# Attention and two feed-forward layers on one core: the work beside the attention in one chunk of 512 tokens per batch instead of two of 288

## The chip, the cores and the metric

The kernel runs on one core of a Trainium2 chip. TensorE multiplies matrices, ScalarE and VectorE evacuate its results, GpSimd works on data in on-chip memory, and SyncE's queue issues nearly all transfers. The metric is the time of one execution on the device in microseconds (us).

## What is computed

Four batches of 576 tokens go through attention with 8 heads of 64, with a decay bias, and then through two feed-forward layers (512 to 2048 to 512) for all 2304 tokens. Cut to what matters:

```python
scores = scale * np.matmul(q, k.transpose(0, 1, 3, 2))
scores = np.where(causal, -1000000000.0, scores + np.minimum(bias, 0.0))
attn = softmax(scores)
x = (attn @ v).transpose(0, 2, 1, 3).reshape(2304, 512)
h = x @ moe_w_in;   x = np.maximum(0.01 * h, h) @ moe_w_out
h = x @ moe2_w_in;  out = (np.maximum(h, 0) + np.log1p(np.exp(-np.abs(h)))) @ moe2_w_out
```

## The kernel before

Every operand of the feed-forward layers is split into a high and a low part, so that a product takes three matmuls. The weights arrive as 64-bit numbers and are loaded and split block by block (`load_w`, `split_w`): a block is 128 of the 2048 inner features, `i` for the first matrix of a layer and `o` for the second. The pool of split weights has 8 places for each kind, and block 8 takes the place of block 0.

The 16 blocks of a layer are worked through in 4 groups of G = 4. The first group of the first layer is special: most of its work is done beside the attention.

The attention works on 16 pairs of heads (four for each batch) in 64 units of scores, four to a pair: rows 384 to 511 (512 columns of scores), the last 64 rows (288), rows 256 to 383 (384), and rows 0 to 255 (256 and 128). They run through a software pipeline. Step n of the loop in `attention` issues the scores of unit n + 1 on TensorE, the maxima and exponentials of unit n, the normalization of unit n - 1 on GpSimd, and the transposes of unit n - 2 on TensorE (`pt_t`) with their evacuation to PA, PZ or PB. In the first and third step of a pair's four (n = 4p, 4p + 2) `pv` multiplies with V (`pt_v`) and splits the result into xh and xl. After the last scores, steps 63 to 66 drain the pipeline.

The class `Fill` holds a queue of units of feed-forward work. When a batch is through the attention, `ready` appends its units; `step` calls `run` in every step of the loop, between the two halves of the transposes, and `run` issues at most one unit: `h` (12 matmuls into `ps_h` for one block) or `o` (12 matmuls into `ps_o` for 128 of the 512 outputs, over the group's four blocks), if the weights and the inputs that it needs are there. A unit's result is evacuated by ScalarE (`gf`, then `gh`) and GpSimd (`gl`), or by ScalarE (`o`), which SyncE's queue stores to `part` in device memory. All units during the attention share one bank of the accumulation memory. From step 64 on, `run` is called more often, and after the loop until the queue is empty.

Then comes the main part: a list of steps, each with an `h` unit for one block and one chunk of tokens, and the output matmuls (`ps_out`) of three steps before. Its first group does what the Fill queue has left, that is the last batch; the next groups work on all tokens in chunks of 512, 512, 256, 512 and 512. `load_acc` brings the stored results of the first group back.

Of the kernel before, what the change touches and what calls it, by code (L numbers as in the profile page):

```python
# [9 lines left out]
F32 = mybir.dt.float32  # L10
I32 = mybir.dt.int32
U32 = mybir.dt.uint32
F32R = mybir.dt.float32r
# [4 lines left out]
P = 128  # L18
NEG = -8.0e9
G = 4  # L20
# [10 lines left out]
def attn_moe_moe(ctx, tc, q, k, v, s, w1i, w1o, w2i, w2o, out):  # L31
    nc = tc.nc

    B, H, S = s.shape
    D = v.shape[-1]
    NT, DM = out.shape
    DFF = w1i.shape[1]
    KD = DM // P
    NF = DFF // P
# [2 lines left out]
    NP = B * NPAIR  # L42
    NB = S // P
    TL = S - NB * P
    CW = S // 2
    scale = 1.0 / float(D) ** 0.5

    nc.scalar.preload_act_table_set("natural_log_exp_and_others")
# [1 line left out]
    def pool(name, bufs=1, **kw):  # L50
        return tc.tile_pool(name=name, bufs=bufs, **kw)

    dram = ctx.enter_context(pool("dram", space=bass.MemoryType.DRAM))
# [4 lines left out]
    xh = keep.tile([P, KD, NT], F32R, tag="xh", name="xh")  # L58
    xl = keep.tile([P, KD, NT], F32R, tag="xl", name="xl")
    bb_d = dram.tile([B * H, 2, S], F32R, tag="bb_d", name="bb_d")  # L60
    part = dram.tile([2 * B, P, KD, CW], F32, tag="part", name="part")


    todo = {}
# [2 lines left out]
    def later(n, fn, *args):  # L67
        todo.setdefault(clock[0] + n, []).append((fn, args))
# [12 lines left out]


    wt, wio = {}, {}
    wpool = ctx.enter_context(pool("wpool", bufs=2 * G))
    wio["tmp"] = ctx.enter_context(pool("wtmp", bufs=2))

    def load_w(layer, f, nm, place=None):
# [10 lines left out]

    def split_w(layer, f, nm, at):

        raw = wt.pop((layer, f, nm, "raw"))
        L, Hw = raw[:, :, 0], raw[:, :, 1]
        m = wio["tmp"].tile([P, DM], I32, tag="wm", name="wm")
        t = wio["tmp"].tile([P, DM], I32, tag="wt", name="wt")
        nc.scalar.activation(m.bitcast(F32), Hw.bitcast(F32), AF.Abs)
        nc.scalar.activation(t, L.bitcast(U32), AF.Copy, scale=2.0 ** -29)

        mf = m.bitcast(F32)

        def clamp():  # L110
            nc.vector.tensor_scalar(mf, mf, D_MIN, D_MAX, op0=ALU.max, op1=ALU.min)

        def shift():
            nc.vector.tensor_scalar(m, m, 3, 0x3FFFFFFF, op0=ALU.logical_shift_left, op1=ALU.bitwise_and)

        def sign():
            nc.vector.scalar_tensor_tensor(m, Hw, -0x40000000, m, op0=ALU.bitwise_and, op1=ALU.bitwise_or)  # L117

        def add():
            nc.gpsimd.tensor_tensor(m, m, t, op=ALU.add)  # L120

        def high():
            hi = wpool.tile([P, DM], F32R, tag=f"w{nm}h", name=f"w{nm}h")
            nc.scalar.activation(hi, m.bitcast(F32), AF.Copy)
            wt[layer, f, nm] = [hi]

        def low():
            lo = wpool.tile([P, DM], F32R, tag=f"w{nm}l", name=f"w{nm}l")
            hi = wt[layer, f, nm][0]
            nc.gpsimd.tensor_tensor(lo, m.bitcast(F32), hi.bitcast(F32), op=ALU.subtract)  # L130
            wt[layer, f, nm].append(lo)

        for n, fn in zip(at, (clamp, shift, sign, add, high, low)):
            later(n, fn)


    def h_mm(ps, layer, f, xh, xl):
        hi, lo = wt[layer, f, "i"]
        n = 0
        for kk in range(KD):  # L140
            w = slice(kk * P, (kk + 1) * P)
            for a, b in ((hi[:, w], xh[:, kk, :]), (hi[:, w], xl[:, kk, :]), (lo[:, w], xh[:, kk, :])):
                nc.tensor.matmul(ps, a, b, start=n == 0, stop=n == 3 * KD - 1)  # L143
                n += 1
# [307 lines left out]
    class Fill:  # L452
# [19 lines left out]
        def step(self, n):  # L472
            if n == 4 * NPAIR + 1:
                self.begin()
            if n in self.loads:
                (f, nm), place = self.loads[n]
                load_w(0, f, nm, wio[place])
            if n - 3 in self.loads:
                split_w(0, *self.loads[n - 3][0], (1, 2, 3, 4, 5, 6))
            self.run()  # L480

        def bank(self, nm):

            tag, bufs = ("m", 1) if not self.free else self.free.pop(0)
            if self.free is not None:
                self.free.append((tag, bufs))
            return self.ps.tile([P, 512], F32, tag=tag, name=nm, bufs=bufs)[:, :CW]

        free = None

# [7 lines left out]
                fn(*args)  # L498

        def ready(self, b):  # L500
            hs, os = [], []
            for ch in range(2):
                c0 = b * S + ch * CW
                x = xh[:, :, c0:c0 + CW], xl[:, :, c0:c0 + CW]
                gs = {}
                hs += [(self.h, (f, x, gs)) for f in range(G)]
                os += [(self.o, (dm, 2 * b + ch, gs)) for dm in range(KD)]

            self.units += hs[:G + 1] + os[:KD] + hs[G + 1:] + os[KD:]

        def h(self, f, x, gs):
            ps = self.bank("ps_h")
            h_mm(ps, 0, f, *x)
            new = lambda pool, nm, dt=F32: pool.tile([P, CW], dt, tag=nm, name=nm)

            def leaky():
                gf = new(self.tpool, "gf")
                nc.scalar.activation(gf, ps, AF.Prelu, alpha=0.01)
                later(1, high, gf)

            def high(gf):
                gh = new(self.gpool, "gh", F32R)
                nc.scalar.activation(gh, gf, AF.Copy)
                later(1, low, gf, gh)

            def low(gf, gh):
                gl = new(self.gpool, "gl", F32R)
                nc.gpsimd.tensor_tensor(gl, gf, gh.bitcast(F32), op=ALU.subtract)
                gs[f] = gh, gl

            later(1, leaky)

        def o(self, dm, c, gs):
            ps = self.bank("ps_o")
            w = slice(dm * P, (dm + 1) * P)
            for f in range(G):
                (wh, wl), (gh, gl) = wt[0, f, "o"], gs[f]
                for n, (a, b) in enumerate(((wh, gh), (wh, gl), (wl, gh))):
                    nc.tensor.matmul(ps, a[:, w], b, start=f == 0 and n == 0, stop=f == G - 1 and n == 2)  # L539

            def store():
                o = self.tpool.tile([P, CW], F32, tag="o", name="o")
                nc.scalar.activation(o, ps, AF.Copy)  # L543
                nc.sync.dma_start(part[c, :, dm, :], o)

            later(1, store)

    with pool("psA", bufs=2, space=PSUM) as psA:
# [11 lines left out]
            tick()  # L560
        fill.stack.close()

    for nm in "io":
        wio[nm] = ctx.enter_context(pool("raw" + nm))
    acc = ctx.enter_context(pool("accpool")).tile([P, KD, NT], F32, tag="acc", name="acc")

    def load_acc(c):
        nc.sync.dma_start(acc[:, :, c * CW:(c + 1) * CW], part[c])


    gpool = ctx.enter_context(pool("gpool", bufs=4, side="right"))
# [2 lines left out]
    ps_o = ctx.enter_context(pool("ps_o", bufs=5, space=PSUM))  # L574

    chunks = [(0, 512), (512, 512), (1024, NT - 2048), (NT - 1024, 512), (NT - 512, 512)]
    first = [((B - 1) * S + ch * CW, CW) for ch in range(2)]
    groups = [(layer, g) for layer in range(2) for g in range(NG)]
    steps = []
    for layer, g in groups:  # L580
# [17 lines left out]
    gs = {}  # L598
# [80 lines left out]
    for gi, (layer, g) in enumerate(groups[1:]):  # L679
        a, z = start[groups[gi]], start[layer, g]  # L680
        when = [(a + n - 1, a + n) for n in (0, 3, 6, 8, 11, 14, 16, 19)] if gi else [None] * 4 + [(0, 2), (1, 4), (3, 6), (5, 8)]
        for j, at in enumerate(when):
            if at:
                f, nm = divmod(j, 2)
                w = (layer, g * G + f, "io"[nm])
                plan.setdefault(at[0], []).append((load_w, w))
                plan.setdefault(at[1], []).append((split_w, (*w, (1, 1, 1, 1, 2, 2))))
    for c in range(2 * (B - 1)):
        plan.setdefault(2 * c + 2, []).append((load_acc, (c,)))

    for n, (layer, g, c, is_first, is_last, f) in enumerate(steps):
        N = c[1]
        cols = slice(c[0], c[0] + N)
        ps = ps_h.tile([P, 512], F32, tag="h", name="ps_h")
        h_mm(ps[:, :N], layer, g * G + f, xh[:, :, cols], xl[:, :, cols])
        tick()
        settle()
        act1(n, layer, N, ps)
        for fn, w in sorted(plan.pop(n, ()), key=lambda x: (split_w, load_w, load_acc).index(x[0])):
            fn(*w)  # L700
        if n >= LAG:
            out_mm(n - LAG)
# [52 lines left out]
```

## Time and profile before

| what | value |
|---|---|
| median of 3 runs | 997.46 us (996.87 to 997.95) |
| the profiled execution: time, span | 996.73 us, 995.0 us |
| TensorE busy | 974.7 us, 98% of the span |
| ScalarE, VectorE, GpSimd busy | 539.2, 526.5, 571.9 us |
| granted clock of TensorE | 1.00 |

A matmul is pipelined: a 512-wide one lasts 390 ns in the profile, while the next one starts after less. So what a stretch costs TensorE is read from the starts of its instructions.

### The profile page before, as it was taken

Reading aid. Unit: us, or ns where it says so; the run is one execution under the profiler, and the core shown is the slowest. Engines: PE = TensorE matmul, PEld = TensorE weight load, DVE = VectorE, ACT = ScalarE, POOL = GpSimd, SP = SyncE. Lnnn points to the kernel's source line nnn. Section 1 sums busy time; section 2 is a strip of 40 time slices with the busy share of each in tenths; the row PEclk is TensorE's granted clock in tenths of the full one; section 3 lists DMA queues with packets and bytes.
Section 4 is the critical chain, followed back from the end, with each engine's and each line's share of the span. In section 5 each row is a group of like instructions: output and inputs, shape, how many; then the busy total and the mean of one; then the engine's idle time right before and its main releaser. Section 6 shows DMA issues by size and latency. Waiting matters only on the chain.

```text
span 995.0 us, 15234 instructions
## 1 busy us (share of the span) xinstructions
PE 974.7 (98%) x5498; PEld 810.8 (81%) x5498; DVE 526.5 (53%) x1133; ACT 539.2 (54%) x1152; POOL 571.9 (57%) x565
## 2 busy tenths in 40 slices
PE   6889999999999999999999999999999999999998
PEld 4667788888898888888888888888888888888886
DVE  6886665545122322132215437767687868763534
ACT  4877766756355333334334546776657655654452
POOL 6757545543256444444444446777867776775553
PEclk9999999999999999999999999999999999999999
DMA  5422324221163111111111111111111111100202
GB/s 176 135 89 80 112 86 132 71 78 32 37 198 127 43 43 43 43 43 43 47 38 43 44 43 42 43 43 43 43 43 43 43 42 43 43 1 1 85 22 85
DMA packets 38519, 62.05 MB, mean 62 GB/s; under 512 B 2932, under 2 KB 25972, under 8 KB 38444
## 3 DMA queue, kind: packets, MB, share of 16 engines
q1 hardware_dynamic: 38204, 60.74, 18.6%
q8 instruction: 44, 0.72, 0.3%
q10 hardware_dynamic: 240, 0.33, 0.1%
q14 instruction: 31, 0.25, 0.1%
HBM read 52.65 MB, written 8.40 MB: 61 GB/s over the span
## 4 chain that ended last, share of the span: by engine, by line
PE 91%; DVE 3%; ACT 3%; issue 1%; POOL 1%; DMA 1%; SPq 0%; ACTq 0%; POOLq 0%; DVEq 0%
PE ps_h L143 40%; PE ps_out L657 36%; PE pt_v L354 4%; PE ps_o L539 4%; PE pt_s L262 3%; PE pt_t L323 3%; PE pt_s L252 1%; ACT sc L295 1%; DVE sc L281 1%; PE pt_t L318 1%; DMA V<-in_v 0%; DVE st L286 0%; ACT PA L335 0%; DVE acc L667 0%; ACT PB L335 0%
## 5 line engine op out<-in xcount | busy, mean ns | idle before, releaser
L150 POOL TENSOR_TENSOR gl<-gf,gh 128x512 fp32r<-128x512 f32 (+2 forms) x148 | 181.1, 1224 | 138.8 <-ACT gh L149 129.1
L143 PE MATMUL ps_h<-xh,wih 128*128 128x512 f32 (+2 forms) x688 | 245.6, 357 | 1.1 <-ACT o L543 0.6
L143 PE MATMUL ps_h<-xl,wih 128*128 128x512 f32 (+2 forms) x688 | 243.8, 354 | 0.0
L143 PE MATMUL ps_h<-xh,wil 128*128 128x512 f32 (+2 forms) x688 | 243.8, 354 | 0.0
L667 DVE TENSOR_TENSOR acc<-ps_out,acc 128x512 f32<-128x512 f32 (+1 forms) x114 | 73.7, 662 | 164.4 <-PE ps_out L657 164.4
L622 POOL TENSOR_TENSOR t<-e,t 128x512 f32<-128x512 f32 (+1 forms) x80 | 112.4, 1406 | 72.0 <-DVE t L621 71.3
L306 POOL TENSOR_SCALAR sc<-sc,st 128x512 f32<-128x512 f32 (+4 forms) x160 | 88.2, 563 | 103.0 <-DVE st L302 60.5
L143 PEld LDWEIGHTS ps_h<-xh,wih 128*128 128x128 f32 x688 | 129.6, 188 | 19.8 <-ACT o L543 0.8
L143 PEld LDWEIGHTS ps_h<-xl,wih 128*128 128x128 f32 x688 | 129.6, 188 | 17.9
L143 PEld LDWEIGHTS ps_h<-xh,wil 128*128 128x128 f32 x688 | 129.5, 188 | 17.6
L606 ACT ACTIVATE gf<-ps_h 128x512 f32<-128x512 f32 (+2 forms) x68 | 36.6, 538 | 170.0 <-PE ps_h L143 169.4
L657 PE MATMUL ps_out<-woh,gl 128*128 128x512 f32 x288 | 112.3, 390 | 0.0
L657 PE MATMUL ps_out<-woh,gh 128*128 128x512 f32 x288 | 112.3, 390 | 0.0
L657 PE MATMUL ps_out<-wol,gh 128*128 128x512 f32 x288 | 112.2, 390 | 0.0
L149 ACT ACTIVATE gh<-gf 128x512 fp32r<-128x512 f32 (+2 forms) x148 | 85.5, 578 | 49.3 <-DVE gf L632 48.6
L295 ACT ACTIVATE sc<-sc,st 128x512 f32<-128x512 f32 (+2 forms) x144 | 83.4, 581 | 42.2 <-DVE st L286 21.2
L120 POOL TENSOR_TENSOR wm<-wm,wt 128x512 int32<-128x512 int32 x64 | 85.0, 1329 | 31.3 <-DVE wm L117 31.3
L657 PE MATMUL ps_out<-gh,wol 128*128 128x512 f32 (+2 forms) x272 | 97.8, 359 | 0.0
L657 PE MATMUL ps_out<-gh,woh 128*128 128x512 f32 (+2 forms) x272 | 97.7, 359 | 0.0
L657 PE MATMUL ps_out<-gl,woh 128*128 128x512 f32 (+2 forms) x272 | 97.7, 359 | 0.0
L281 DVE CUSTOM_DVE_ANT_0 sc<-pt_s,mask 128x512 f32<-128x512 f32 (+2 forms) x144 | 66.7, 480 | 57.0 <-PE pt_t L323 46.0
L621 DVE TENSOR_SCALAR t<-e 128x512 f32<-128x512 f32 (+1 forms) x80 | 44.3, 554 | 98.0 <-ACT e L612 98.0
(93 smaller groups left out, 1731.7 us busy)
## 6 DMA issues: line engine op xcount, KB each, us to landing
rawi<-in_moe_w_in SPq DMA_DIRECT2D x32, 512.0 KB
rawo<-in_moe_w_out SPq DMA_DIRECT2D x32, 512.0 KB
V<-in_v SPq DMA_DIRECT2D x16, 320.0 KB
Q<-in_q SPq DMA_DIRECT2D x15, 320.0 KB
K<-in_k SPq DMA_DIRECT2D x16, 288.0 KB
out<-acc SPq DMA_DIRECT2D x18, 256.0 KB
part<-o SPq DMA_DIRECT2D x24, 144.0 KB
acc<-part SPq DMA_DIRECT2D x6, 576.0 KB
```

The lines of the kernel that those rows point to most:

```text
L120: nc.gpsimd.tensor_tensor(m, m, t, op=ALU.add)
L143: nc.tensor.matmul(ps, a, b, start=n == 0, stop=n == 3 * KD - 1)
L149: nc.scalar.activation(gh, gf, AF.Copy)
L150: nc.gpsimd.tensor_tensor(gl, gf, gh.bitcast(F32), op=ALU.subtract)
L281: nc.vector.tensor_tensor_reduce(out=self.sc[:, j, c], in0=self.ps[j][:, c], in1=m, scale=-scale, scalar=3.0e38, op0=ALU.add, op1=ALU.min, ...
L295: nc.scalar.activation(x, x, AF.Exp, scale=-1.0, bias=self.stat(0, e), accum_out=self.stat(1, e))
L306: nc.gpsimd.tensor_scalar(x, x, self.stat(2, e), 1.0, op0=ALU.mult, op1=ALU.mult)
L354: nc.tensor.matmul(pt[j * D:(j + 1) * D, o:o + w], V[p % 2][:, c, j, :], x[:, j, :], start=m == 0 or (not last and m == 1), stop=m == len( ...
L621: nc.vector.tensor_scalar(t, e, 1.0, -1.0, op0=ALU.add, op1=ALU.add)
L622: nc.gpsimd.tensor_tensor(t, e, t, op=ALU.subtract)
L657: nc.tensor.matmul(ps, a, b, start=f == 0 and m == 0, stop=f == G - 1 and m == 2)
L667: nc.vector.tensor_tensor(d, o, d, op=ALU.add)
```

## The change

A batch's turn at the Fill queue is one chunk of 512 tokens instead of two of 288: chunk b is the tokens 512 b to 512 b + 511, released when batch b is through. Three batches release 24 units of 512 instead of 48 of 288. The main part's first group takes the 768 tokens that are left, in two chunks of 384, instead of 576 in two of 288. Tiles of the units grow from 288 to 512 columns. The pool of split weights becomes two, of six places and of two; the second is made only behind the attention. Each block has the same turn among 8 places as before.

```diff
-    CW = S // 2
+    FW = 512
...
-    part = dram.tile([2 * B, P, KD, CW], F32, tag="part", name="part")
+    part = dram.tile([B - 1, P, KD, FW], F32, tag="part", name="part")
...
-    wpool = ctx.enter_context(pool("wpool", bufs=2 * G))
+    wpools = [ctx.enter_context(pool("wpool0", bufs=6))]
...
+        wp = wpools[(layer * NF + f) % (2 * G) // 6]
...
-            hs, os = [], []
-            for ch in range(2):
-                c0 = b * S + ch * CW
-                x = xh[:, :, c0:c0 + CW], xl[:, :, c0:c0 + CW]
-                gs = {}
-                hs += [(self.h, (f, x, gs)) for f in range(G)]
-                os += [(self.o, (dm, 2 * b + ch, gs)) for dm in range(KD)]
-
-            self.units += hs[:G + 1] + os[:KD] + hs[G + 1:] + os[KD:]
+            c, gs = slice(b * FW, (b + 1) * FW), {}
+            x = xh[:, :, c], xl[:, :, c]
+            self.units += [(self.h, (f, x, gs)) for f in range(G)] + [(self.o, (dm, b, gs)) for dm in range(KD)]
...
+    wpools.append(ctx.enter_context(pool("wpool1", bufs=2)))
...
-        nc.sync.dma_start(acc[:, :, c * CW:(c + 1) * CW], part[c])
+        nc.sync.dma_start(acc[:, :, c * FW:(c + 1) * FW], part[c])
...
-    first = [((B - 1) * S + ch * CW, CW) for ch in range(2)]
+    n0 = (B - 1) * FW
+    n1 = (NT - n0) // 2
+    first = [(n0, n1), (n0 + n1, n1)]
...
-    for c in range(2 * (B - 1)):
+    for c in range(B - 1):
         plan.setdefault(2 * c + 2, []).append((load_acc, (c,)))
```

The order of TensorE's instructions at step 44, the first step of the twelfth pair, before:

```order
L252 MATMUL pt_s<-BK_91,BQ_89 128x288
L323 MATMUL pt_t<-ident,sc 128x128 x3
L143 MATMUL ps_h<-xh,wih 128x288
L143 MATMUL ps_h<-xl,wih 128x288
L143 MATMUL ps_h<-xh,wil 128x288
...
L354 MATMUL pt_v<-PA,V_92 64x192 x8
L354 MATMUL pt_v<-PZ,V_92 64x64 x2
L262 MATMUL pt_s<-K_87,Q_85 128x384 x2
```

And of the change:

```order
L253 MATMUL pt_s<-BK_91,BQ_89 128x288
L324 MATMUL pt_t<-ident,sc 128x128 x6
L355 MATMUL pt_v<-PA,V_92 64x192 x8
L355 MATMUL pt_v<-PZ,V_92 64x64 x2
L263 MATMUL pt_s<-K_87,Q_85 128x384 x2
```

The unit between the two halves of the transposes is gone there, and so it is in steps 45 to 50; each batch has eight units in place of sixteen.

TensorE at the end of the attention (the last transposes, the last multiplication with V and what follows it), before:

```order
L323 MATMUL pt_t<-ident,sc 128x128 x3
L539 MATMUL ps_o<-gh,woh 128x288
L539 MATMUL ps_o<-gl,woh 128x288
...
L354 MATMUL pt_v<-PB,V_93 64x128 x2
L354 MATMUL pt_v<-PB,V_93 64x256 x4
...
L539 MATMUL ps_o<-gh,wol 128x288
L143 MATMUL ps_h<-xh,wih 128x288
L143 MATMUL ps_h<-xl,wih 128x288
```

And of the change:

```order
L355 MATMUL pt_v<-PA,V_93 64x192 x8
L355 MATMUL pt_v<-PZ,V_93 64x64 x2
L324 MATMUL pt_t<-ident,sc 128x128 x6
L355 MATMUL pt_v<-PB,V_93 64x128 x2
L355 MATMUL pt_v<-PB,V_93 64x256 x4
L144 MATMUL ps_h<-xh,wih 128x384
L144 MATMUL ps_h<-xl,wih 128x384
```

The 13 units that stood between and behind the last steps are gone; the main part's first unit, 384 wide, follows at once.

## Rows read from the trace of the kernel before

**Rows 1.** The page: span, TensorE's busy time, the chain's shares by engine

```profile
span 995.0 us, 15234 instructions
...
PE 974.7 (98%) x5498; PEld 810.8 (81%) x5498; DVE 526.5 (53%) x1133; ACT 539.2 (54%) x1152; POOL 571.9 (57%) x565
...
PE 91%; DVE 3%; ACT 3%; issue 1%; POOL 1%; DMA 1%; SPq 0%; ACTq 0%; POOLq 0%; DVEq 0%
```

**Rows 2.** Table of stretches: start:end, length, each engine's busy time; seven steps each

```profile
165.50:196.26 30.76, 30.76 (x257) 25.89 (x255) 18.45 (x69) 20.58 (x59) 18.09 (x27) 1.00 0.21 70
90.41:112.17 21.76, 20.80 (x174) 15.00 (x172) 17.69 (x69) 16.69 (x48) 14.85 (x23) 1.00 0.31 104
45.73:69.83 24.10, 20.35 (x173) 14.65 (x172) 20.20 (x72) 17.98 (x50) 15.25 (x23) 1.00 0.29 92
```

**Rows 3.** Waits of TensorE, 45.73 to 69.83 us: total, times, longest

```profile
PE pt_t L323 <- ACT PB L335: 2.1, 2, 1.2
PE pt_t L323 <- DVE PZ L337: 1.1, 2, 0.8
```

**Rows 4.** Timeline of TensorE around a unit: start, duration

```profile
166.98 0.38 PE L143 MATMUL ps_h<-xh,wih 128*128 128x288 f32 x1
...
168.64 0.27 PE L323 MATMUL pt_t<-ident,sc 128*128 128x128 f32 x1
```

**Rows 5.** Timeline of TensorE, twelve 512-wide matmuls of the main part

```profile
317.00 0.39 PE L657 MATMUL ps_out<-gh,woh 128*128 128x512 f32 x1
...
319.72 0.39 PE L143 MATMUL ps_h<-xh,wih 128*128 128x512 f32 x1
```

**Rows 6.** Timeline of TensorE, twelve 288-wide matmuls of the main part

```profile
281.46 0.29 PE L657 MATMUL ps_out<-gh,woh 128*128 128x288 f32 x1
...
283.04 0.30 PE L143 MATMUL ps_h<-xh,wih 128*128 128x288 f32 x1
```

**Rows 7.** Table of stretches: single steps and steps 60 to 62, 24 to 26

```profile
174.03:179.12 5.09, 5.09 (x50) 4.35 (x49) 2.62 (x13) 3.35 (x9) 3.17 (x6) 1.00 0.00 0
...
141.36:144.91 3.55, 3.55 (x38) 2.75 (x37) 2.91 (x11) 3.18 (x10) 1.76 (x3) 1.00 0.01 5
...
99.83:101.98 2.15, 2.08 (x13) 1.05 (x12) 1.27 (x6) 2.03 (x7) 1.24 (x3) 1.00 0.45 130
...
86.92:90.41 3.49, 3.49 (x25) 2.67 (x24) 2.37 (x7) 3.38 (x10) 1.81 (x3) 1.00 0.67 221
144.91:148.38 3.47, 3.47 (x26) 2.65 (x25) 3.14 (x12) 3.04 (x11) 1.17 (x2) 1.00 0.31 94
...
232.69:246.31 13.62, 13.62 (x119) 11.59 (x117) 6.70 (x29) 7.80 (x20) 5.66 (x11) 1.00 0.04 12
90.41:99.83 9.42, 9.07 (x82) 6.82 (x81) 7.88 (x31) 7.21 (x21) 7.92 (x11) 1.00 0.22 79
```

**Rows 8.** Table of stretches: from the end of step 62 to the main part

```profile
246.31:275.04 28.73, 27.00 (x212) 25.01 (x210) 4.26 (x13) 11.99 (x33) 7.42 (x12) 1.00 0.11 37
```

**Rows 9.** Timeline of the drain and behind it, engine by engine

```profile
250.09 1.64 POOL L306 TENSOR_SCALAR sc<-sc,st 128x256 f32<-128x256 f32 x4 [0.61 <-DVE PZ L337]
...
255.50 0.27 PE L323 MATMUL pt_t<-ident,sc 128*128 128x128 f32 x1
...
256.02 0.56 DVE L337 COPY PB<-pt_t 128x384 f32<-128x384 f32 x1 [1.68 <-PE pt_t L323]
...
259.09 1.52 PE L354 MATMUL pt_v<-PB,V 128*64 128x128 f32 x16
...
260.66 0.49 ACT L361 ACTIVATE xh<-pt_v 128x384 fp32r<-128x384 f32 x1 [1.00 <-PE pt_v L354]
...
261.18 0.56 DVE L365 TENSOR_TENSOR xl<-pt_v,xh 128x384 fp32r<-128x384 f32 x1 [4.60 <-ACT xh L361]
...
275.04 0.40 PE L143 MATMUL ps_h<-xh,wih 128*128 128x288 f32 x1 [0.55 <-ACT o L543]
...
275.51 0.38 SPq L91 DMA_DIRECT2D rawi<-in_moe_w_in  x1
...
280.66 0.66 ACT L105 ACTIVATE wm<-rawi 128x512 f32<-128x512 f32 x1
```

More of the change, by code (lines that the diff above doesn't have):

```diff
@@ L122, in high @@
         def high():
-            hi = wpool.tile([P, DM], F32R, tag=f"w{nm}h", name=f"w{nm}h")
+            hi = wp.tile([P, DM], F32R, tag=f"w{nm}h", name=f"w{nm}h")
             nc.scalar.activation(hi, m.bitcast(F32), AF.Copy)
@@ L127, in low @@
         def low():
-            lo = wpool.tile([P, DM], F32R, tag=f"w{nm}l", name=f"w{nm}l")
+            lo = wp.tile([P, DM], F32R, tag=f"w{nm}l", name=f"w{nm}l")
             hi = wt[layer, f, nm][0]
@@ L486, in bank @@
                 self.free.append((tag, bufs))
-            return self.ps.tile([P, 512], F32, tag=tag, name=nm, bufs=bufs)[:, :CW]
+            return self.ps.tile([P, 512], F32, tag=tag, name=nm, bufs=bufs)
         free = None
@@ L513, in h @@
             h_mm(ps, 0, f, *x)
-            new = lambda pool, nm, dt=F32: pool.tile([P, CW], dt, tag=nm, name=nm)
+            new = lambda pool, nm, dt=F32: pool.tile([P, FW], dt, tag=nm, name=nm)
             def leaky():
@@ L541, in store @@
             def store():
-                o = self.tpool.tile([P, CW], F32, tag="o", name="o")
+                o = self.tpool.tile([P, FW], F32, tag="o", name="o")
                 nc.scalar.activation(o, ps, AF.Copy)
```

## Prediction

> **What bounds the kernel now.** I read the page first. TensorE is busy for 974.7 of 995.0 us and 91% of the chain that ended last is TensorE's own work [rows 1], so a change counts by what it does to TensorE's stretch of issue and to its 20 us of waits. The profiled execution took 996.73 us, 1.73 more than its span and 0.73 below the median of the runs (997.46); I work out a difference and put it on the median. A measurement of this kernel can tell about 0.2%, 2.0 us, from no change.
>
> Then I read tables of stretches whose edges are the starts of attention steps. The same seven steps of the attention loop stand there three times [rows 2]: steps 44 to 50 with a unit of the Fill queue in each take 30.76 us and TensorE has no idle time; steps 24 to 30 without any unit take 21.76 us, of which it works 20.80; steps 12 to 18, earlier and also without units, take 24.10 and it works 20.35. So a filled step is bound by TensorE, and an unfilled one by the other engines: what TensorE waits for there is evacuations of transposes, PB by ScalarE and PZ by VectorE [rows 3]. A unit in a step costs less than it takes: (30.76 - 21.76) / 7 = 1.29 us each, against 1.66 us from its first matmul to the next transpose (166.98 to 168.64) [rows 4]. The reader is to see that units are worth something only in steps that would wait, and one per step was what the queue gave.
>
> **The change, part by part.** By the order of instructions, units now stand in steps 19 to 22, 31 to 38, 40 to 43, 51 to 54 and 56 to 59, 24 of them, 512 wide. Before, 35 of 48 units stood in steps 19 to 62 and 13 came after step 62, whose end is 246.31 us.
>
> *Wider units.* Twelve 512-wide matmuls issue in 2.72 us (317.00 to 319.72) [rows 5]; with the small first gap of a unit behind transposes 2.74. Against 1.66 [rows 4] that is +1.08 us for each of the 23 steps that held a unit before too: +24.8 us (1.05 to 1.12 each). Here a rule speaks for far more. The Trainium skill, page "TensorE: Matmul & The Clock Gate", section "Back-to-back issue gap", gives a sustained spacing of about 131 ns for 512 columns in streams of weight loads and matmuls. By it a unit would be an estimated 12 x 131 ns = 1.57 us, and 24 units some 28 us less than I count. The trace does not agree: 227 ns each [rows 5].
>
> *Step 38* had no unit and takes 3.55; a filled step of its kind takes 5.09, so 5.09 + 1.08 - 3.55 = +2.6 us [rows 7]. *Steps 23 and 39* lose theirs: 3.49 and 3.47 become the 2.15 of an unfilled one, -2.7 us [rows 7].
>
> *Steps 44 to 50* lose all seven. They have the kinds of steps 24 to 30 and two weight splits at the same places (steps 23 and 28 there, 43 and 48 here), so I price them by that row: 21.76 - 30.76 = -9.0 us. Bounds: -10.0 if TensorE never waits (20.80), -6.7 at the price of the early steps (24.10) [rows 2]. The early ones hold three splits, which is why I take the nearer row. Steps 24 to 30 themselves stay as they are, between -1.0 and +2.3 by the same rows.
>
> *Steps 60 to 62* lose three: 13.62 becomes 9.42, as steps 24 to 26, -4.2 us (9.07, if no wait is left; 10.4 if they stretch as 24.10 does to 21.76) [rows 7].
>
> Up to the end of step 62: 24.8 + 2.6 - 2.7 - 9.0 - 4.2 = +11.5 us.
>
> *The drain.* From 246.31 to the first matmul of the main part at 275.04 there are 28.73 us, with 13 units and 1.7 us of idle [rows 8]. None of the units is left, so it becomes the latency of the last unit of the attention. GpSimd ends its normalization at 250.09 + 1.64, 5.42 us after step 62; it stood behind no unit's work for long, so I keep that. Then its second transposes, 0.52 us until VectorE copies (255.50 to 256.02), 0.56 for the copy, 1.57 from the last pt_v matmuls to ScalarE's xh (259.09 to 260.66), 0.52 to VectorE's xl and 0.56 for it [rows 9], and some 0.2 for three handovers: 9.4 us. The last two count because the first matmul of the main part waited, at 275.04, for the evacuation before it (0.55 us, ScalarE's o) [rows 9], though its operands were long there; without such a wait it would be 8.1, since the first nine matmuls of a unit don't need the last pair of heads. The other end is the pace of an unfilled pair, 12.34 us from 99.83 to 112.17 [rows 2, 7] plus the 1.2 to xl, 13.5. I take 9.4, the same chain in this very place: -19.3 us.
>
> *The main part's first group* does 768 tokens, not 576: 16 units of 12 matmuls, 384 wide. 288 wide they issue in 1.58 us for twelve (281.46 to 283.04), 131.7 ns each [rows 6], 512 wide in 227. No matmul of 384 is in the trace; between the two 172.5 ns on a line, 170 by the price per column of the wide one and 176 by that of the narrow one. I take 173: 192 x (173 - 131.7) = +7.9 us (7.4 to 8.4).
>
> *Edits that I cost at nothing.* The evacuations of a unit get longer as its matmuls do; in filled steps ScalarE is the fullest of the others, 20.58 of 30.76 [rows 2], and its step grows by 1.08 us. The store of a unit's output and its load later move the same bytes per token and hide behind TensorE. The weights' pools keep eight places in the same turn, and the last two are first written behind the attention, as before; only if the load of the first of these blocks landed later than its split starts would ScalarE hold up the main part. That load is issued at 275.51 in the trace and ScalarE's split of it starts at 280.66, 5.15 us later [rows 9]; from the drain's end there are three units of 12 x 173 ns = 2.1 us ahead of the split, 6.2 us, so the cover holds, and without it the cost would be those 5.15 us at most.
>
> Sum: +11.5 - 19.3 + 7.9 = +0.1 us, 997.6 us; I give 997.5. The move pays with one hand what it takes with the other: 192 tokens go from steps that could cover part of them to a place where nothing does, and a tail of 13 units that was pure TensorE time goes away.
>
> **Rivals.** *Slower: the unfilled steps wait as the early ones do.* They then cost 24.10 rather than 21.76 for seven, in two stretches, and 10.4 rather than 9.42 for three: +2.3 + 2.3 + 1.0 = +5.6 us, 1003.1; at half of that 1000.3. It decides from about a third, that is from 22.6 us for seven steps. For it: the waits are for ScalarE and VectorE [rows 3], and a 512-wide unit leaves them more to do just ahead of the first unfilled step. Against it: three splits against two. *A slow drain* alone (13.5 us) gives +4.2, 1001.7. *Faster: the unfilled steps don't wait*, since the other engines catch up during the long units ahead: -1.0, -1.0 and -0.35, that is 995.2. For it: steps 24 to 26, just behind filled ones, idle only 9.42 - 9.07 = 0.35 us; against it: the four steps after them idle another 0.6 [rows 2, 7]. With a drain of 8.1 as well it is 993.9. *Faster: wide matmuls cost less in a unit than in the main part.* By rows the least is 1.05 rather than 1.08 for each, -0.7 us, which decides nothing. The Trainium skill's figure above would be this rival's large form; the trace bears it out nowhere.
>
> **How the numbers follow.** Forecast (within 2.0 us of 997.5): 0.56. Slower by unfilled steps 0.17, by the drain 0.05. Faster by unfilled steps without waits, alone or with the short drain, 0.21; by cheaper wide matmuls 0.01. So faster 0.22, same 0.56, slower 0.22. The range takes in the short drain with no waits (993.9) nearly whole and half of the slow rival (1000.3): 994.3 to 1000.7; beyond it I leave 0.1 on each side.
>
> **What would show it.** In the profile after: units of 2.74 us in the attention and TensorE without idle in their steps; steps 44 to 50 in 21.8 us and 60 to 62 in 9.4, with waits for PB and PZ; step 62's end 11.5 us later, at 257.8; main part's first matmul 9.4 us behind it; 33.2 us for the first group's 16 units; from there on as before. It is wrong if the seven steps take more than 22.6 or the drain more than 11.3 us, or if both fall to their floors.

## The result, and the profile after

The changed kernel takes 1002.78 us (median of 6 runs, 1001.76 to 1004.38) against 997.41 (6 runs): ratio 1.0057, 95% interval 1.0047 to 1.0068. The forecast was 997.5, within 994.3 to 1000.7; the change is slower by 5.4 us, and the side that the forecast gave 0.22 came true. Its runs stand in two groups: 1001.8 to 1002.0 us, and 1003.5 to 1004.4 with the granted clock at 0.997 in place of 0.999. The profiled execution, 1002.03 us, is of the first group; the second has a section of its own below.

The page of the changed kernel answers to [rows 1]:

```profile
span 1000.2 us, 14564 instructions
...
PE 974.3 (97%) x5210; PEld 795.7 (80%) x5210; DVE 528.1 (53%) x1133; ACT 534.9 (53%) x1116; POOL 569.6 (57%) x553
...
PE 89%; DVE 4%; ACT 4%; issue 1%; POOL 1%; DMA 1%; SPq 0%; ACTq 0%; POOLq 0%; DVEq 0%
```

TensorE is as busy as before (974.3 against 974.7 us). The span grew by 5.2 us, and all of it is time in which TensorE waits: 20.3 us before, 25.9 now. The chain shows it too: TensorE 89% for 91%, VectorE and ScalarE 4% each for 3%.

A table of stretches (start:end, length, busy time of TensorE, weight load, VectorE, ScalarE, GpSimd): steps 24 to 30, 32 to 38, 44 to 50 and 60 to 62, the drain, and the main part up to its first 512-wide `h`:

```profile
93.81:117.64 23.83, 20.87 (x173) 15.00 (x172) 19.47 (x71) 17.59 (x49) 15.41 (x23) 1.00 0.35 117
122.28:161.25 38.97, 38.97 (x257) 30.20 (x256) 18.59 (x69) 22.49 (x54) 15.67 (x24) 1.00 0.25 83
185.21:207.45 22.24, 20.75 (x173) 14.99 (x171) 17.98 (x69) 15.85 (x43) 14.13 (x22) 1.00 0.33 109
253.23:262.23 9.00, 9.00 (x82) 6.81 (x80) 6.51 (x29) 5.97 (x15) 4.11 (x9) 1.00 0.08 29
262.23:272.02 9.79, 6.23 (x55) 4.30 (x53) 4.25 (x13) 4.52 (x14) 2.63 (x6) 1.00 0.01 2
272.02:299.20 27.18, 27.18 (x157) 27.18 (x157) 5.81 (x9) 13.32 (x28) 14.10 (x12) 1.00 0.63 214
```

Against [rows 2, 7, 8] the terms of the forecast's sum come out so (the last but one is what the span leaves):

| term | forecast, us | measured, us |
|---|---|---|
| *Wider units* (23 steps) | +24.8 | +26.9 |
| *Step 38* | +2.6 | +2.7 |
| *Steps 23 and 39* | -2.7 | -2.7 |
| *Steps 24 to 30 stay as they are* | 0 | +2.1 |
| *Steps 44 to 50* | -9.0 | -8.5 |
| *Steps 60 to 62* | -4.2 | -4.6 |
| *The drain* | -19.3 | -18.9 |
| *First group* | +7.9 | +8.2 |
| sum, from span to span | +0.1 | +5.2 |

In the last stretch TensorE has no idle time, as forecast. Two terms of 2.1 us each make most of the miss. The first is read from one unit; a timeline of TensorE in step 58, start and duration:

```profile
243.76 0.47 PE L534 MATMUL ps_o<-gh,woh 128*128 128x512 f32 x1
244.07 0.39 PE L534 MATMUL ps_o<-gl,woh 128*128 128x512 f32 x1
...
246.38 0.39 PE L534 MATMUL ps_o<-gh,wol 128*128 128x512 f32 x1
246.61 0.60 PE L324 MATMUL pt_t<-ident,sc 128*128 128x128 f32 x4
```

The unit takes 246.61 - 243.76 = 2.85 us, not 2.74. The gap behind its first matmul is 0.31 us, and the ten after it take (246.38 - 244.07) / 10 = 231 ns each, where the main part's rows give 227 [rows 5]. Seven filled steps show the same: (38.97 - 30.76) / 7 = 1.17 us each.

The second is read from TensorE's waits in steps 24 to 30 (total, times, longest):

```profile
PE pt_t L324 <- DVE PZ L338: 1.5, 1, 1.5
PE pt_t L324 <- ACT PB L336: 1.4, 2, 0.9
```

The wait of 1.5 us stands in step 24, which takes 5.21 us instead of 3.63. The other 0.5 us stand in step 26 (4.46 for 3.96), where the longer of the two waits for PB is 0.9 us instead of 0.5; step 46, its like among steps 44 to 50, grows by the same 0.5. From step 19 up to step 24 only the units' price was off.

### The profile page after: what moved, and what is told of

It is laid out like the page before. It is cut to its first block, busy times and chain, and to the rows that moved or that the text cites. A ratio compares the mean times of both kernels' runs of the same rounds, so it can differ in the third digit from the quotient of the medians.

```text
span 1000.2 us, 14564 instructions
## 1 busy us (share of the span) xinstructions
PE 974.3 (97%) x5210; PEld 795.7 (80%) x5210; DVE 528.1 (53%) x1133; ACT 534.9 (53%) x1116; POOL 569.6 (57%) x553
## 4 chain that ended last, share of the span: by engine, by line
PE 89%; DVE 4%; ACT 4%; issue 1%; POOL 1%; DMA 1%; SPq 0%; ACTq 0%; POOLq 0%; DVEq 0%
PE ps_h L144 40%; PE ps_out L655 36%; PE pt_v L355 4%; PE ps_o L534 3%; PE pt_t L324 3%; PE pt_s L263 2%; ACT sc L296 2%; DVE sc L282 1%; PE pt_s L253 1%; DVE st L287 1%; PE pt_t L319 0%; DMA V<-in_v 0%; ACT PA L336 0%; ACT PB L336 0%; ACT xh L362 0%
## 5 line engine op out<-in xcount | busy, mean ns | idle before, releaser
L144 PE MATMUL ps_h<-xh,wih 128*128 128x512 f32 (+2 forms) x640 | 236.6, 370 | 1.2 <-DVE xl L366 1.2
L144 PE MATMUL ps_h<-xl,wih 128*128 128x512 f32 (+2 forms) x640 | 235.7, 368 | 0.0
L144 PE MATMUL ps_h<-xh,wil 128*128 128x512 f32 (+2 forms) x640 | 235.7, 368 | 0.0
L144 PEld LDWEIGHTS ps_h<-xh,wih 128*128 128x128 f32 x640 | 120.6, 188 | 21.1 <-DVE xl L366 1.4
L144 PEld LDWEIGHTS ps_h<-xl,wih 128*128 128x128 f32 x640 | 120.6, 188 | 19.6
L144 PEld LDWEIGHTS ps_h<-xh,wil 128*128 128x128 f32 x640 | 120.5, 188 | 19.5
```

## Which part of the change costs

**The pools alone.** The kernel before with `wpool` split in `wpool0` (6) and `wpool1` (2), and nothing else of the change.

> The kernel before with only the pools of split weights made two, of six places and of two. If the slowdown comes from the chunks (all theories but one): 997.4, within 0.5 us of before. If it came from where the pools lie in memory or from the later second pool: about 1002.8.

Measured: 996.89 us, 0.9996 (0.9987 to 1.0005). The pools cost nothing.

**The tokens alone.** The changed kernel, but each batch's 512 tokens as two chunks of 256, in the unit order of the kernel before; the main part's first group does 768 tokens, as in the change:

```diff
-            c, gs = slice(b * FW, (b + 1) * FW), {}
-            x = xh[:, :, c], xl[:, :, c]
-            self.units += [(self.h, (f, x, gs)) for f in range(G)] + ...
+            for ch in range(2): ...      # 256 tokens each
+            self.units += hs[:G + 1] + os[:KD] + hs[G + 1:] + os[KD:]
```

> The changed kernel, but the 512 tokens of a batch as two chunks of 256 in the order of before: 48 units again, the main part's first group with 768 tokens as in the change. Theory of the empty steps (the loss is TensorE idle in unfilled steps and in an uncovered drain): units stand where they stood before, no wait comes back; 48 units get cheaper by 0.12 to 0.14 us each (12 x (131.7 - 120 ns)), -6.2 us, the first group costs +8.2: 999.4. Rival, the moved tokens cost it all (8.2 us for 192 tokens at full price, the rest a wash): about 1002 to 1003, since only columns count. Rival, 512-wide matmuls are the loss: also below 1000, but then unfilled steps of the change would show no wait.

Measured: 997.57 us, 1.0004 (0.9995 to 1.0013), 1.8 us better than expected. From the main part's first matmul on, the profile gives 7.9 us more than before (727.8 for 719.9), as expected of the 192 tokens; from step 19 up to there it gives 7.5 us less (197.7 for 205.2), which is 0.16 us for each of the 48 units. So the tokens that moved and the 384-wide matmuls are no loss in sum. What costs is that the same columns stand in 24 units rather than 48, so that half the steps have nothing for TensorE to do while the others work: its waits up to 275 us add up to 15.5 us here and 15.1 before, but to 21.0 in the changed kernel.

## Step 24: what made TensorE wait

My first theory was the load that a wide unit leaves: its 512-wide `gh` and `gl` beside the split of the seventh weight, whose instructions VectorE takes in turn with the attention's. Four kernels bear on it.

**The split moved earlier**, by the key of its load (the split starts three steps later):

```diff
-            self.loads = dict(zip((0, 2, 5, 8, 11, 15, 20, 25, ...
+            self.loads = dict(zip((0, 2, 5, 8, 11, 15, 19, 25, ...     # one step; and 17, three steps
```

> The changed kernel with the seventh load of the attention one step earlier, so that its split falls into step 22, which holds a unit, and not into step 23, which holds none. Theory of the split in an empty step: step 24 loses its wait of 1.5 us, total -1.6 us, about 1001.2. Rival, the wait in step 24 comes from the 512-wide evacuation of the unit of step 22 alone: no change, 1002.8.

> The changed kernel with the seventh load three steps earlier, so that its split starts in step 20 and nearly all of it lies in filled steps. The earlier run with the split one step earlier left most of its VectorE and GpSimd work in steps 23 and 24 and moved nothing. Theory: of the 1.6 us that step 24 takes more than before (5.21 against 3.63), 1.0 is the split and 0.6 the evacuation of the 512-wide unit ahead (step 56 of the run with held units takes 4.26 without any split): step 24 in 4.3 us, total -1.0, about 1001.8. Rival, the unit's evacuation alone: step 24 stays at 5.2.

Measured: one step earlier 1002.89 us, 1.0059 (1.0046 to 1.0071), step 24 at 5.46 us, a miss: the split's work on VectorE and GpSimd still lay in steps 23 and 24. Three steps earlier 1000.92 us, 1.0032 (1.002 to 1.0045); step 24 takes 4.26 us, and steps 24 to 30 take 21.94, as good as the 21.76 of before [rows 2]:

```profile
94.58:116.52 21.94, 20.81 (x172) 15.00 (x171) 17.15 (x68) 15.98 (x46) 12.20 (x22) 1.00 0.38 126
```

So the 2.1 us need the split in these steps, though step 24 alone stays 0.6 us above its 3.63 (step 26, at 3.55, makes up for it). But the kernel before had the same split in the same steps.

**`gl` on VectorE.** In step 24 of the changed kernel VectorE's clamp of the weight (L112) takes 1.06 us, instead of 0.57 before, and ends 0.28 us behind GpSimd's `gl`, as it does before; so `gl` was given to VectorE:

```diff
-                nc.gpsimd.tensor_tensor(gl, gf, gh.bitcast(F32), op=ALU.subtract)
+                nc.vector.tensor_tensor(gl, gf, gh.bitcast(F32), op=ALU.subtract)
```

> The changed kernel with the units' gl computed on VectorE and not on GpSimd. If step 24 is long because VectorE's clamp of the weight is held until GpSimd's 512-wide gl ends, step 24 falls from 5.2 to about 4.3 us, VectorE's 0.6 us for each of 12 gl hides in filled steps, and the time is 1000.5 to 1001 us. If it is the amount of work that ScalarE and VectorE have behind a wide unit, VectorE's gl makes it worse: step 24 stays at 5.2 or above, and the time is 1002.1 us or more.

Measured: 1004.59 us, 1.0065 (1.0053 to 1.0078), four of its five runs in the group near 1004 us; the one at a clock of 0.999 took 1001.92. Step 24 takes 5.10 us. The clamp now takes 0.42 us, but VectorE's own `gl` ahead of it 0.68, and 0.42 + 0.68 is 1.10: the run does not tell the two causes apart, and it made me read the rows of step 24 again.

Timeline of the changed kernel from step 23 on (ScalarE, VectorE, TensorE in order of start), and below it the three rows of the kernel before that answer to its clamp, scores and copy of PZ:

```profile
93.52 0.62 ACT L518 ACTIVATE gh<-gf 128x512 fp32r<-128x512 f32 x1
93.81 0.65 PE L253 MATMUL pt_s<-K,Q 128*128 128x288 f32 x2
...
94.73 1.06 DVE L112 TENSOR_SCALAR wm<-wm 128x512 f32<-128x512 f32 x1 [0.40 <-ACT wm L106]
...
95.71 0.68 DVE L282 CUSTOM_DVE_ANT_0 sc<-pt_s,mask 128x512 f32<-128x512 f32 x1
...
96.61 0.25 DVE L338 COPY PZ<-pt_t 64x128 f32<-64x128 f32 x1
...
97.01 0.52 PE L324 MATMUL pt_t<-ident,sc 128*128 128x128 f32 x3 [1.47 <-DVE PZ L338]
```

```profile
89.81 0.57 DVE L111 TENSOR_SCALAR wm<-wm 128x512 f32<-128x512 f32 x1 [0.22 <-ACT wm L105]
...
90.41 0.65 PE L252 MATMUL pt_s<-K,Q 128*128 128x288 f32 x2
...
91.63 0.25 DVE L337 COPY PZ<-pt_t 64x128 f32<-64x128 f32 x1
```

The reader is to see where TensorE's first scores of step 24 stand in VectorE's chain. From the scores of step 23 (91.66 now, 86.92 before [rows 7]) to the copy of PZ VectorE needs 4.95 us now and 4.71 before: 0.24 more. But the scores of step 24 come 2.80 us ahead of that copy now and 1.22 before: 1.58 more, just what step 24 grew by. TensorE got there early, since step 23 no longer holds a unit (2.15 for 3.49 us, the -1.34 that the sum took as a gain).

**A unit in step 23.** So the first batch's four `h` units were moved by one step, from 19 to 22 to 20 to 23; a wide unit then leaves its evacuations even nearer to step 24.

```diff
-            self.run()
+            if n != 19:
+                self.run()
```

> The changed kernel with the first batch's four h units in steps 20 to 23 and not 19 to 22; nothing else moves. First theory: step 24 is long because step 23 lost the unit that covered the evacuations and the weight's split ahead of VectorE's copy of PZ; the copy came 1.2 us behind the start of step 24 before and 2.8 us behind it now, while VectorE's work up to it grew by only 0.24 us. Then step 24 falls from 5.21 to about 3.8 us, step 23 becomes 4.64, step 19 becomes 2.15, and the first group of runs moves from 1002.0 to about 1000.6 us. Rival: step 24 is long because a wide unit leaves ScalarE, VectorE and GpSimd more to do. Then a wide unit in step 23 leaves even more, step 24 stays at 5 us or above, and the time is 1002 us or more.

Measured, the row of step 23, and that of steps 24 to 30:

```profile
90.39:95.04 4.65, 4.65 (x26) 3.28 (x25) 2.88 (x7) 4.35 (x13) 2.31 (x3) 1.00 0.64 208
95.04:117.23 22.19, 20.90 (x173) 14.99 (x172) 17.55 (x69) 16.47 (x44) 15.31 (x23) 1.00 0.27 93
```

Step 24 takes 3.63 us as before the change, although VectorE's clamp is held there by `gl` for 1.08 us too. The rival, which wanted 5 us or more, falls, and the lost cover is shown. It also costs without the split, but less: step 56 of the next kernel below, behind a step 55 without a unit and far from any split, takes 4.26 us, as step 24 does with the split moved away, and step 44, behind a unit, 3.63. Step 26 stays at 4.44 us with the unit in step 23; why it and step 46 take 0.5 us more than before was not separated. From the start of step 19 to the end of step 62 the profile gives 190.76 us against 192.40 of the changed kernel, -1.64. The median did not follow as far: 1001.8 us, 1.0043 (1.003 to 1.0057), for 1000.6 expected. In its profile step 1 starts at 14.87 us, in that of the changed kernel at 13.73, and these 1.14 us take most of the 1.64 back (1001.57 us for this execution, 1002.03 for that one). That time lies between 13.55 and 14.88 in the 18 profiles of this study. TensorE's rows show where it comes from: the same two scores matmuls ahead of step 1, in the changed kernel and below it in this one, take

```profile
13.16 0.65 PE L253 MATMUL pt_s<-BK,BQ 128*128 128x288 f32 x2
```

```profile
13.77 1.17 PE L253 MATMUL pt_s<-BK,BQ 128*128 128x288 f32 x2
```

The ratio, 1.8, is about that of the multiplication of PA with V in the drain of two executions below: 2.83 us with TensorE's clock at its lower level, 1.52 at its upper one. So the clock probably came up later in this execution; the column of the granted clock reads 1.00 there in both and does not show it. The starts of the runs that were not profiled are not known.

## The drain, and units spread over the steps

**Units held for the drain.** The last four units are not issued in steps 56 to 59, but in steps 63, 64 and 65 and behind the last `pv`:

```diff
-            self.run()
+            if not 56 <= n < 63 and n != 66:
+                self.run()
...
-            if n >= len(units):
+            if n == len(units) + 2:
                 fill.run()
```

> The changed kernel with the last four units of the third batch held back from steps 56 to 59 and issued in steps 63, 64, 65 and behind the last multiplication with V. Theory of the uncovered drain: steps 55 to 62 get 9.6 us shorter, the drain 7.8 us longer (four units of 2.85, of which some 3.6 us lie in waits that are there now), so -1.8 us, 1001.0. Rival, the drain is a latency that units in it only lengthen: -9.6 + 11.4 = +1.8 us, 1004.6. If the lower clock that half of the runs of the change show comes from the drain, it is gone in this kernel's runs and their spread falls below 1 us.

Measured: 1001.48 us, 1.0041 (1.0029 to 1.0054). From the end of step 62 to the main part 18.44 us pass with four units of 2.85 in them, so 7.04 without, against 9.79. But a wait came back: step 56, which now stands without a unit behind a step 55 that has none either, takes 4.26 us, where step 44, behind a filled step, takes 3.63.

**Units in even steps alone**, which puts one into every step that waited:

```diff
-            self.run()
+            if n % 2 == 0 or n > 62:
+                self.run()
```

> The changed kernel with a unit in every second step only (the even ones), so that units stand in steps 20 to 26, 32 to 38, 40 to 46, 48 to 54 and 56 to 62, and the last four in the drain. Theory of the empty steps: a 512-wide unit gives the other engines enough time for its own step and the next, the waits of 2.0 and 1.4 us in steps 24 to 30 and 44 to 50 go, and 2.8 us of the drain's idle: 6 us less than the change, 996 to 997, level with before or under it. Rival, a step without a unit waits whatever stands ahead of it (2.15, 3.63, 1.82, 4.46 us as in the change): only the drain gains, about 1001.

Measured: 1000.33 us, 1.0026 (1.0015 to 1.0038), less than half of what was expected. The steps with units wait little (6.31 us in most), but step 58 takes 7.20, and the drain still waits 1.4 us for PA and 1.2 for `xl`.

**Both, and the earlier split.** Even steps, the drain's places and load key 17 together; then the drain's places and key 17 without the even steps; then these two and the first units in steps 20 to 23.

> The changed kernel with units in even steps alone, the seventh weight's split begun in step 20 and the last units at the drain's waits (steps 63, 64, 65 and behind the last pv). If waits are what is lost and the three remedies add up: even steps gave 1000.33; the drain's placement took 1.0 us off (19.43 to 18.44 us for the same four units), the earlier split should take the idle time of 70 to 120 us from 1.5 to 1.0: 998.8 us, still above the kernel before, since its 0.9 us wait of step 58 and one of the drain's stay. If the remedies cover the same waits, or the wait moves to another step, it stays at 1000.3.

> The changed kernel with the seventh weight's split begun in step 20 and the last four units held to steps 63, 64, 65 and behind the last pv. The two remedies gave 1000.92 and 1001.48 us one by one, against 1002.1 and 1002.8 of the changed kernel: if they add, 1000.1 us; if the second part only moves the wait to step 56 (4.26 us there), 1000.9 us.

> The same with the seventh weight's split begun in step 20 and the last four units held for the drain, which gave 999.57 us with the h units in steps 19 to 22. If the unit in step 23 covers what is left there (step 24 at 4.26 us, against 3.63 of the kernel before), 999.0 us; if nothing is left to cover, 999.6 us. In neither case below the kernel before.

Measured: 1002.4 us, 1.0049 (1.0035 to 1.0063), worse than the even steps alone; 999.57 us, 1.002 (1.0011 to 1.0028), where the two savings add up; and 1000.1 us, 1.0029 (1.0019 to 1.0039), no better. In the first the wait moved: the split's instructions now run from step 20 to step 23, and step 22, which has a unit, takes 7.78 us instead of 6.31. Step 26, behind the split, takes 7.20 instead of 6.47, for a reason that no run here separates. A row of TensorE's waits over these steps:

```profile
PE pt_t L324 <- ACT PB L336: 1.5, 2, 0.9
```

In the third, step 24 fell to 3.63 us as it should (4.26 without), but step 21 rose from 4.58 to 5.20 and step 26 from 3.55 to 4.47. None of these kernels beats the kernel before. The best still has 2 us more of TensorE's waits up to 275 us than it (17.3 for 15.1).

## Why some runs take 2 us more

The changed kernel ran again three times, as it is:

> The changed kernel once more, for its spread beside the others on the same chip: 1001.8 to 1004.4, in two groups 2 us apart, by the mean granted clock of 0.999 and 0.997. If the drain lets the clock fall, a profiled execution of the second group shows a granted clock below 1.00 behind 262 us; if not, the lower clock lies at the start or the end.

> The changed kernel once more, for its second group of runs, near 1004 us at a granted clock of 0.997. If this execution is one of them: a low granted clock in the middle of the kernel, of some 4 us, which by the first theory follows the idle time of step 24 (94 to 100 us from the start) and by its rival that of the drain (262 to 272 us). If it is one of the first group, 1002.0 us and no fall of the clock before the end, which tells nothing.

> The changed kernel once more on the same chip, for how often its clock falls there: two or three of five runs at 1003.5 to 1004.5 us and a granted clock of 0.997, the others at 1001.8 to 1002.2.

Measured: 1002.1 us (1.0052, 1.0039 to 1.0064; two of five runs at 0.997); one run of 1004.57 us at 0.997; 1004.33 us (1.0064, 1.0052 to 1.0077; three of five at 0.997). With the first six runs that is 9 of 17. The single run was profiled. A table of stretches of 1 us from 263 us on, the drain; the column behind GpSimd's is TensorE's granted clock:

```profile
263.00:264.00 1.00, 0.80 (x8) 0.42 (x4) 0.22 (x1) 0.74 (x2) 1.00 (x2) 1.00 0.00 0
264.00:265.00 1.00, 0.00 (x0) 0.00 (x0) 1.00 (x6) 1.00 (x6) 0.14 (x1) 1.00 0.00 0
265.00:266.00 1.00, 0.67 (x4) 0.42 (x4) 0.49 (x1) 0.97 (x5) 0.00 (x0) 1.00 0.00 0
266.00:267.00 1.00, 0.45 (x4) 0.33 (x3) 0.52 (x3) 0.49 (x1) 0.42 (x1) 0.92 0.00 0
267.00:268.00 1.00, 1.00 (x7) 0.59 (x7) 0.51 (x1) 0.00 (x0) 1.00 (x4) 0.50 0.00 0
...
270.00:271.00 1.00, 1.00 (x12) 0.88 (x8) 0.18 (x1) 0.35 (x2) 0.00 (x0) 0.87 0.00 0
```

The clock is at its upper level up to 266 us and at 0.50, its lower one, from 267 to 270; the drain takes 11.41 us instead of 9.79. Up to the end of step 62 this execution and the first one differ only by their start. Of the 2.6 us between their spans the start makes 0.87 and the drain 1.62, so it is in the drain that the clock falls and not in step 24, which I had expected. The clock fell between 266 and 267 us, behind the longest wait there, in which TensorE does nothing from about 263.8 to 265.1 (for PA, 1.4 us).

**TensorE kept busy.** Two kernels add matmuls of 512 columns whose result nothing reads: 14 behind steps 64 to 66 and the last `pv`; or six in step 63, inside that wait.

```diff
+            if n == 63:
+                ps = self.bank("ps_x")
+                for k in range(6):
+                    nc.tensor.matmul(ps, xh[:, 0, :P], xh[:, k % KD, :FW], ...)
```

> The changed kernel with 14 more matmuls of 512 columns at the waits of the drain (behind steps 64 to 66 and the last pv); their result is read by nothing, so they only keep TensorE busy. Fourteen by 0.227 us are 3.2 us in waits of some 2.5 us: 0.5 to 0.8 us more than the first group of the changed kernel's runs (1002.0). If the runs near 1004 us are those in which the granted clock fell in the drain because TensorE idled there, none of these runs shows 0.997: 1002.5 to 1002.8 us, all within 1 us. If the clock falls for a reason other than the idle time, or at that place anyway, two of five runs lie 1.6 to 2 us above the others.

> The changed kernel with six more matmuls of 512 columns in step 63 alone, between the last transposes L319 and L315, where TensorE waits 1.4 us for ScalarE's PA; their result is read by nothing. 6 x 0.227 = 1.36 us fill that wait almost exactly. If the granted clock falls because of that wait, it now stays at its upper level in every run: no run near 1004 us, all at 1001.8 to 1002.6. If the thin work of the whole drain (262 to 272 us) lets it fall, some of the runs still lie 1.6 to 2 us above the others.

Measured: the 14 give 1005.55 us, 1.0075 (1.006 to 1.0089), three of five runs at 0.998; in its profile the clock is at 0.75 in the stretch from 266 to 267 us, before all but two of the added matmuls. They came too late, and cost more than expected: its two runs without the fall take 1003.2 and 1003.6 us. The six give 1002.22 us (1001.83 to 1002.78), 1.0052 (1.0038 to 1.0065), none of five below 0.999, on the chip on which the unchanged one showed three of five. Its drain takes 9.79 us, and the clock stays up all through it:

```profile
262.00:264.00 2.00, 2.00 (x20) 1.47 (x17) 1.02 (x7) 1.43 (x6) 1.09 (x2) 1.00 0.03 8
264.00:266.00 2.00, 1.82 (x9) 0.98 (x7) 1.48 (x7) 1.89 (x9) 0.06 (x1) 1.00 0.00 0
266.00:268.00 2.00, 1.45 (x16) 1.14 (x17) 1.00 (x4) 0.49 (x1) 1.50 (x4) 1.00 0.00 0
```

At 9 of 17, five runs without a fall would come by chance in (8/17)^5 = 2% of cases. The wait in step 63 is what lets the clock fall, as far as five runs can show it. It does not do so alone. Seven profiles have this wait unfilled and at its place: step 1 starts at 13.66, 13.73 and 14.12 us in the three without a fall (the changed kernel twice, and the split one step earlier, of whose five runs one other is near 1004 us) and at 14.42, 14.50, 14.60 and 14.88 in the four with one (the 14 added matmuls, the changed kernel twice, `gl` on VectorE). So the fall goes with a late start; the profile with the six matmuls, which starts at 14.53, shows none. The kernels with the split in step 20 and with the unit in step 23 have the same wait and, in their profiles, a late start (14.51 and 14.87), but no run of theirs (five each) is of this kind; there the wait comes 1.5 to 1.9 us sooner after step 1. Why the time of the wait matters is open.

## Why the prediction was wrong

*What bounds the kernel.* Right: TensorE's issue and its waits. Filled steps stay without idle time, and the loss against the kernel before is all waits; of the miss against the forecast 2.1 us are waits that were not forecast and 2.1 us are TensorE's own time. None of the signs that the forecast named for being wrong came up (22.24 us against 22.6, 9.79 against 11.3); the unit's price and steps 24 to 30, where the two misses lie, were not among these signs.

*Steps 24 to 30 themselves stay as they are.* This is the step that failed by mechanism. The term for step 23 was priced at what the unit takes, -1.34 us, and its neighbour at no change. But the unit was the cover of ScalarE's and VectorE's work for step 24; without it -1.34 came back there as +1.58, and step 26 added 0.5, whose cause is open. The working asks of each edit what work hides it, and did not ask it of the removed unit. The slower rival ("the unfilled steps wait as the early ones do") had the right place here, and its price for these seven steps, +2.3, was near; its reason, that a wide unit leaves the others more to do, explains 0.24 of the 1.58 us (VectorE's 4.95 for 4.71). At its two other places it did not come true: steps 44 to 50, where step 43 keeps its unit, take 22.24 us against a turning point of 22.6, and steps 60 to 62 take 9.00, less than forecast.

*Wider units.* The mechanism was right and the size off: 1.17 us each, not 1.08, outside the stated 1.05 to 1.12. The price was made from the main part's steady 227 ns; inside the attention a unit's matmuls come every 231 ns and the first gap is 0.31. Times 23 that is 2.1 us. Why the matmuls are slower there was not tried. The Trainium skill, page "TensorE: Matmul & The Clock Gate", section "Back-to-back issue gap", gives about 131 ns for 512 columns; no row here, at any place of the kernel, agrees with it.

*The drain.* 9.79 us for 9.4, and its first matmul waited for VectorE's `xl`, as said. What the forecast did not ask is what the idle time in that chain, 1.4 us of it in step 63, does to the clock: 1.6 us in about half of the runs, which no rival had.

*First group.* A matmul of 384 columns is where the line between the measured widths put it, (282.56 - 280.48) / 12 = 173 ns:

```profile
280.48 0.33 PE L655 MATMUL ps_out<-gh,woh 128*128 128x384 f32 x1
...
282.56 0.33 PE L144 MATMUL ps_h<-xh,wih 128*128 128x384 f32 x1
```

## What to carry to other kernels

Filler work beside a chain that waits was worth the number of steps that it covers here, not its columns: the same tokens in units half as wide cost nothing (1.0004), in wide ones 0.6% (1.0057). When a unit is taken out of a step, price the next step too, by how far the other engines' chain is behind TensorE without it. And of a stretch that loses its cover, ask whether TensorE still works enough in it to keep its clock.

## What the runs showed of the hardware

VectorE's instructions can be held until one of GpSimd ends. `st<-st`, a subtraction of 128x1, takes 158 ns where it is alone; in the changed kernel's timeline it starts 0.2 us behind GpSimd's `gl` and ends with it:

```profile
151.64 1.10 DVE L287 TENSOR_TENSOR st<-st 128x1 f32<-128x1 f32 x1
```

```profile
151.44 1.28 POOL L523 TENSOR_TENSOR gl<-gf,gh 128x512 fp32r<-128x512 f32 x1
```

With `gl` on VectorE the same instruction takes 0.16 us. The Trainium skill states this on the page "SBUF — State Buffer", section "SBUF: two separate sides": the port pair that both engines share is an exclusive lock for a whole instruction. The trace agrees, down to an instruction of one column. Here it decided nothing, as the unit in step 23 showed.

The clock's fall cost 1.6 us (a drain of 11.41 us for 9.79) behind a wait of 1.4. The Trainium skill, page "TensorE: Matmul & The Clock Gate", section "Part 1: The HAM clock gate", says that the clock is set by how busy TensorE has been recently. The rows of the drain agree: the lower level follows the idle stretch, and with the wait filled the clock stayed at 1.00.
